# Attention's q·kv as three float32r products with a block-diagonal kv, partial sums kept in PSUM, and the maximum of k as a tree: one change to a Trainium2 kernel

## The chip, the cores and the metric

The kernel runs on one core of one Trainium2 chip. The metric is the device time of one execution in microseconds; shown are the median, the lowest and the highest of three runs. Engines are named as the profile names them: PE (matrix products), PEld (its weight loads), DVE (vector), ACT (scalar), POOL (GpSimd) and SP (which issues the DMAs).

## The reference

The kernel computes a linear attention whose softmax of q runs over the head dimension and whose softmax of k runs over the sequence, and then two feed-forward blocks. There are 8 batches of 8 heads, 576 positions and 64 head dimensions; 4608 tokens, a width of 512 and 2048 hidden units.

```
q_s = softmax(q, axis=-1); k_s = softmax(k, axis=2)
kv = np.einsum('bhsd,bhse->bhde', k_s, v)
attn = np.einsum('bhsd,bhde->bhse', q_s, kv)
x = attn.transpose(0, 2, 1, 3).reshape(B * S, H * D)
h = x @ w_in; x = (h * (1.0 / (1.0 + np.exp(-1.702 * h)))) @ w_out
h = x @ w_in2; out = np.maximum(0.01 * h, h) @ w_out2
```

## The kernel before

**Tiles and halves.** Tokens go in nine chunks of 512 (0 to 8). Matrix products of the two feed-forward blocks (`layer` 0 and 1) take float32r operands in two halves, a high and a low one: `split_hi` (L83) rounds on ACT, `split_lo` (L86) subtracts on DVE, and each product is a sum of three, high·high, low·high and high·low.

**Stages.** First, attention of chunk 0 in an order written out by hand (`FIRST`). Then a loop over the 16 tiles of hidden units (and five more turns) does the first matrix of layer 0 for chunks 0 and 1 (`g1`, L719), the second (`g2`, L789), and converts the weights, which come as 64-bit words (`c1` to `c4`). Attention of chunk 1 runs in its first turns, and chunks 2 and 3 in the turns after, one unit in two turns. Then come pairs of chunks (0,2), (0,4), (0,6), the single chunk (0,8), and layer 1 with the pairs (1,0), (1,2), (1,4), (1,6) and the single (1,8). A pair's first matrix is a product of 2 by 2 blocks with seven block products instead of eight (`quad_step`, and `quad_apart` from (1,2) on; L732): eight steps for a pair, 32 by `quad_step` and 24 by `quad_apart`. The second matrix is `g2`, or from (1,2) on seven rounds in `pair_apart` (L1056).

**A step of a pair.** It has three PSUM banks a, b and c (tag `h`, names `ha`, `hb`, `hc`). The products go, six matmuls each, in the order a = a11·w11; b = s2·t2; c = s1·t1; a += a12·w21; b += s3·t3; c += s4·w22; b += a22·t4. ACT copies a's first product to SBUF (`p1`), and DVE adds it to what later comes out of b and c, so a step has five DVE adds (L900 and its helper, L956 in `quad_apart`). Pieces of other work stand in ten gaps of a step.

**Attention in units.** A unit is a chunk and a pair of heads (c, j), four to a chunk; `Units.tick` puts its pieces into the gaps of three successive steps. `k1` takes k's maximum over rows with a reduction (L429), and with a further maximum for what is left over in chunk 0 (L431). `k6` multiplies k and v into the bank `kvp`, and `k7` divides by the sum on ACT into `kv` (L492), three buffers for each j. `q3` transposes the scaled q, `q4` copies it to `qT` (L540). `x_product` (L556) multiplies kv and qT: for each of the two heads a float32 matmul on a 64 by 64 quarter of the array, and since batches of 576 positions don't fall on chunks of 512, chunks 1 to 7 have two pieces each (64 and 448 columns in chunk 1, 128 and 384 in chunk 2, and so on). Chunks 0 and 8 have one piece of 512. From the pairs on, `kma`, `kmb`, `qtp`, `kvp` and `pxt` of the units share one PSUM bank (tag `att`).

**Order.** Each engine runs its queue in order. The order is set by a scheduler from the program's text; the gaps are where the text puts the pieces. The lines that call `x_product` stand in `tick`:

```
if c:
    at(0, x_product, *c)
    at(0, self.done, *c)
```

Of the kernel before, what the change touches and what calls it, by code (L numbers as in the profile page):

```python
# [26 lines left out]
def tile_softmax_linear_attention_two_mlps(  # L27
# [247 lines left out]
    def sums_hi(n):  # L275
        h = pool["wt"].tile([P, 4, 2 * P], F32R, tag="wt", name="wt", bufs=1)
        split_hi(sums[n][1], h)
        sums[n].append(h)

    def sums_lo(n):  # L280
        _, t, h = sums.pop(n)
        lo = t.bitcast(F32R)
        split_lo(t, h, lo)
        for i, half in enumerate((h, lo)):
            nc.sync.dma_start(out=wtd[:, :, n, i, :], in_=half.bitcast(F32))
# [111 lines left out]
    def load_first(p0):  # L397

        def slot(name):
            return p0.tile([P, 4 * T], F32, tag=name, name=name)  # L400
# [4 lines left out]
        va, vb = slot("va"), slot("vb")  # L405
# [20 lines left out]
    def k1(b, j):  # L426
        km, *rest = kin[b, j]
        mx = sb.tile([P, 2, D], F32, tag="kmx", name="kmx", bufs=2)
        nc.vector.tensor_reduce(out=mx, in_=km.rearrange("p h r d -> p h d r"), axis=AX.X, op=ALU.max)  # L429
        for kr in rest:  # L430
            nc.vector.tensor_tensor(out=mx, in0=mx, in1=kr, op=ALU.max)  # L431
        kst[b, j] = mx

# [52 lines left out]
    def k7(b, j):  # L486
# [29 lines left out]
    def q2(c, j):  # L516
        qt, sm = qin.pop((c, j)), qst[c, j]
        nc.vector.reciprocal(sm, sm)
        qs = sb.tile([P, R, 2, D], F32, tag="qs", name="qs", bufs=3)
# [17 lines left out]
    def q4(c, j):  # L537
        pt = qst.pop((c, j))
        t = sb.tile([P, T], F32, tag="qs", name="qT", bufs=3)
        nc.scalar.copy(t, pt)  # L540
        qT[c, j] = t
# [3 lines left out]
    def x_product(c, j):  # L545
        t = qT.pop((c, j)).rearrange("p (r c) -> p r c", r=R)
# [3 lines left out]
        while done < T:  # L550
# [3 lines left out]
            for h in range(2):  # L554
                o = slice(h * D, (h + 1) * D)
                nc.tensor.matmul(pv[o, :, a:e], kvb[b, j][o, :], t[o, :, a:e], start=True, stop=True)  # L556
# [284 lines left out]
    class Units:  # L841
# [8 lines left out]
        def tick(self):  # L850
# [8 lines left out]
            if c:  # L859
                at(0, x_product, *c)  # L860
                at(0, self.done, *c)
# [32 lines left out]
    def quad_step(layer, n, gaps, extra):  # L894
# [7 lines left out]
        a = ps.tile([P, T], F32, tag="h", name="ha", bufs=3)  # L902
# [608 lines left out]
```

## Time and profile before

| what | value |
|---|---|
| median of 3 runs | 1627.37 us (1627.02 to 1627.89) |
| profiled execution, its own time | 1628.65 us |
| its span, first to last instruction | 1626.9 us |
| PE busy | 1587.7 us, 98% of the span |
| DVE busy | 1053.7 us, 65% |
| ACT busy | 800.9 us, 49% |
| granted clock of PE, mean | 0.997 of full speed |

The profiled execution took 1.75 us more than its span, and 1.3 us more than the median. Busy time is the union of an engine's instructions. A matmul's end is modelled and overlaps the start of the next, so the durations of single matmuls are no price for one in a dense row: their distance from start to start is.

### The profile page before, as it was taken

What the parts mean: (1) busy time and instruction counts of PE and PEld (TensorE: products, weight loads), DVE (VectorE), ACT (ScalarE), POOL (GpSimd) and SP (SyncE); (2) the same over time, 40 slices, a digit from 0 to 9 for tenths busy, and PEclk for the clock granted to TensorE, in tenths of its full rate; (3) what the DMA queues carried; (4) which work ended last, traced back from release to release, by engine and by line L of the source; (5) the groups of instructions that cost most, each with busy time, mean ns of one, the idle gap of its engine ahead of it and who ended that gap; (6) DMA issues with size and microseconds to landing.
All of it is one profiled execution on the core that took longest, in us unless ns stands there. A gap on an engine that the chain in (4) does not pass through costs nothing.

```text
span 1626.9 us, 22121 instructions
## 1 busy us (share of the span) xinstructions
PE 1587.7 (98%) x7632; PEld 1268.3 (78%) x7632; DVE 1053.7 (65%) x1623; ACT 800.9 (49%) x1698; POOL 35.2 (2%) x162
## 2 busy tenths in 40 slices
PE   5999999999999999999999999999999999999998
PEld 3677778777877778778888888788888888888887
DVE  7899659786776757667544666644774487547411
ACT  7787656556545655445333545333453354334422
POOL 1000000000000002000000000000000000000000
PEclk9999999999999999999999999999999999999999
DMA  8788577778788887978896977996776777676763
GB/s 215 226 274 256 167 234 269 255 247 262 249 281 264 260 260 243 303 253 281 306 330 228 321 272 264 316 292 203 242 209 203 233 212 215 194 230 195 223 192 102
DMA packets 221775, 397.84 MB, mean 245 GB/s; under 512 B 57568, under 2 KB 138464, under 8 KB 221664
## 3 DMA queue, kind: packets, MB, share of 16 engines
q1 hardware_dynamic: 221664, 396.43, 76.1%
q8 instruction: 61, 1.00, 0.3%
q14 instruction: 50, 0.41, 0.1%
HBM read 306.18 MB, written 90.18 MB: 244 GB/s over the span
## 4 chain that ended last, share of the span: by engine, by line
PE 77%; DVE 7%; DMA 7%; issue 3%; ACT 1%; SPq 1%; ACTq 0%; DVEq 0%; POOL 0%; POOLq 0%
PE acc L789 23%; PE hb L732 13%; PE ha L732 9%; PE hc L732 8%; PE h L719 7%; PE ob L1056 6%; PE oa L1056 4%; PE oc L1056 4%; DMA o<-cv 2%; PE pxt L556 2%; DMA wo<-wp 1%; DMA w<-cv 1%; DVE cv L126 1%; DVE gl L86 1%; DMA raw<-in_moe_w_in_dram 1%
## 5 line engine op out<-in xcount | busy, mean ns | idle before, releaser
L789 PE MATMUL acc<-gh,wo 128*128 128x512 f32 x1152 | 362.8, 396 | 2.6 <-ACT wo L83 1.8
L789 PEld LDWEIGHTS acc<-gh,wo 128*128 128x128 f32 x1152 | 211.5, 188 | 48.9 <-ACT wo L83 2.2
L789 PE MATMUL acc<-gl,wo 128*128 128x512 f32 x576 | 225.6, 392 | 0.0
L719 PE MATMUL h<-x,wi 128*128 128x512 f32 x768 | 191.3, 399 | 2.8 <-ACT wi L83 2.8
L719 PEld LDWEIGHTS h<-x,wi 128*128 128x128 f32 x768 | 144.2, 191 | 37.2 <-ACT wi L83 4.4
L732 PE MATMUL ha<-x,wa 128*128 128x512 f32 x624 | 161.8, 393 | 2.8 <-ACT p L905 2.8
L732 PEld LDWEIGHTS ha<-x,wa 128*128 128x128 f32 x624 | 115.6, 188 | 33.0 <-issue 5.7
L83 ACT CAST sh<-a 128x1024 fp32r<-128x1024 f32 x84 | 88.2, 1050 | 94.4 <-PE oc L1056 35.1
L86 DVE TENSOR_TENSOR sl<-a,sh 128x1024 fp32r<-128x1024 f32 x84 | 102.7, 1222 | 49.4 <-ACT sh L83 49.0
L789 PEld LDWEIGHTS acc<-gl,wo 128*128 128x128 f32 x576 | 108.3, 188 | 23.8 <-issue 0.8
L956 DVE TENSOR_TENSOR a<-hb,a 128x512 f32<-128x512 f32 x72 | 49.7, 690 | 91.3 <-PE hb L732 91.3
L732 PE MATMUL hb<-x,wc 128*128 128x512 f32 x384 | 97.4, 389 | 0.0
L508 ACT ACTIVATE qt<-qt,qmx 128x64 f32<-128x64 f32 x256 | 86.0, 338 | 13.0 <-DVE qmx L498 12.2
L1056 PE MATMUL ob<-sh,wo 128*128 128x512 f32 x288 | 91.7, 394 | 0.0
L732 PE MATMUL hb<-xb,wb 128*128 128x512 f32 x336 | 86.1, 390 | 0.0
L83 ACT CAST gh<-gb 128x512 fp32r<-128x512 f32 x80 | 49.3, 617 | 71.8 <-PE acc L789 69.6
L732 PEld LDWEIGHTS hb<-x,wc 128*128 128x128 f32 x384 | 72.1, 188 | 14.9
L789 PE MATMUL acc<-wo,gh 128*128 128x512 f32 x256 | 79.2, 390 | 1.3 <-DMA wo<-wp 1.3
L83 ACT CAST gh<-gf 128x512 fp32r<-128x512 f32 x96 | 59.1, 616 | 42.5 <-DVE gf L757 33.6
L86 DVE TENSOR_TENSOR gl<-gb,gh 128x512 fp32r<-128x512 f32 x80 | 54.7, 687 | 35.5 <-ACT gh L83 34.2
L86 DVE TENSOR_TENSOR gl<-gf,gh 128x512 fp32r<-128x512 f32 x96 | 65.9, 687 | 18.0 <-ACT gh L83 17.1
L753 ACT ACTIVATE a<-a 128x512 f32<-128x512 f32 x72 | 45.5, 632 | 64.2 <-DVE a L956 64.2
(182 smaller groups left out, 2842.2 us busy)
## 6 DMA issues: line engine op xcount, KB each, us to landing
wo<-wo SPq DMA_DIRECT2D x144, 512.0 KB, 4.6
wo<-wp SPq DMA_DIRECT2D x68, 512.0 KB, 3.6
wo<-wt SPq DMA_DIRECT2D x48, 512.0 KB, 3.6
wa<-wq SPq DMA_DIRECT2D x40, 512.0 KB, 4.0
wb<-wq SPq DMA_DIRECT2D x40, 512.0 KB, 4.2
wc<-wq SPq DMA_DIRECT2D x40, 512.0 KB, 4.7
raw<-in_moe_w_in_dram SPq DMA_DIRECT2D x32, 512.0 KB, 4.9
raw<-in_moe_w_out_dram SPq DMA_DIRECT2D x32, 512.0 KB, 4.9
```

The lines of the kernel that those rows point to most:

```text
L83: nc.scalar.copy(hi, src)
L86: nc.vector.tensor_tensor(out=lo, in0=src, in1=hi.bitcast(F32), op=ALU.subtract)
L126: nc.vector.scalar_tensor_tensor(out=w[:, o], in0=hw, scalar=0xC0000000, in1=w[:, o], op0=ALU.bitwise_and, op1=ALU.bitwise_or)
L508: nc.scalar.activation(t[:, h, r, :], t[:, h, r, :], AF.Exp, bias=mx[:, h, r : r + 1], accum_out=sm[:, h, r : r + 1],)
L556: nc.tensor.matmul(pv[o, :, a:e], kvb[b, j][o, :], t[o, :, a:e], start=True, stop=True)
L719: nc.tensor.matmul(h, WI[f][:, b, wh, o * P : (o + 1) * P], xs[f"a{side}{b + 1}"][xh][:, o, :], start=(i == 0), stop=(i == n - 1),)
L732: nc.tensor.matmul(h, w[:, wh, o * P : (o + 1) * P], xo[xh][:, o, :], start=(start and i == 0), stop=(i == 5), skip_group_check=not start,)
L753: nc.scalar.activation(t, h, AF.Prelu, alpha=0.01)
L789: nc.tensor.matmul(acc[d], lhsT, rhs, start=(f == 0 and i == 0), stop=(f == NF - 1 and i == 2))
L956: add = lambda out, h, t: nc.vector.tensor_tensor(out=out, in0=h, in1=t, op=ALU.add)
L1056: nc.tensor.matmul(banks[name][d], w[:, l, wh, sl], x[:, l, :], start=first_one, stop=(m == NQ // 2 - 1 and l == 1 and i == 2), skip_group ...
```

## The change

Three things are changed.

**q·kv.** For chunk 0 all stays. For chunks 1 to 8, `k7` writes kv of two heads as the two diagonal blocks of a 128 by 128 tile, in a high half (two ACT instructions of 64 by 64) and a low half (two DVE instructions); eight such tiles (`kvt`, two batches by four j) are set to zero once by POOL. kv of batch 0, which chunk 1 needs too, is split by `k8` after `FIRST` (eight ACT and eight DVE instructions of 64 by 64). `q4` writes qT as a high half (ACT) and a low half (DVE). `x_product` is then three float32r matmuls over the whole array for each piece: high·high, low·high, high·low. In `tick` it moves from gap 0 to gap 1.

**Sums in PSUM.** In a step, ACT copies a's first product into bank b, in PSUM; the order of the next two is exchanged (c = s1·t1, then b += s2·t2), and b adds onto the copy. ACT then copies c and b to SBUF (`v5`, `u2`). Of the five DVE adds two remain; ACT has three copies instead of one. The seven rounds of `pair_apart` change in the same way. Three matmuls are added ahead of the first pair, one into each bank `h`.

**Maximum of k.** One reduction is replaced by a maximum of 256 elements, one of 128, and one of 128 for the rest.

Buffers are moved for room: the converted weights have three shared buffers (`cv`) instead of two and two; `qs` has two instead of three; the pool `wt` is gone, and `sums_hi` and `sums_lo` use the room of the new halves of qT, so the first does two ACT casts instead of one and the second three DMAs instead of two.

```diff
     def c1(i, f):
-        t = pool["cv"].tile([P, 2, T], U32, tag=f"cv{i}", name="cv", bufs=2)
+        t = pool["cv"].tile([P, 2, T], U32, tag="cv", name="cv", bufs=3)
...
     def k1(b, j):
         km, *rest = kin[b, j]
+        kr = rest[0] if rest else km[:, :, R, :]
         mx = sb.tile([P, 2, D], F32, tag="kmx", name="kmx", bufs=2)
-        nc.vector.tensor_reduce(out=mx, in_=km.rearrange("p h r d -> p h d r"), axis=AX.X, op=ALU.max)
-        for kr in rest:
-            nc.vector.tensor_tensor(out=mx, in0=mx, in1=kr, op=ALU.max)
+        two = sb.tile([P, 2, R // 2, D], F32, tag="km2", name="km2", bufs=1)
+        nc.vector.tensor_tensor(out=two, in0=km[:, :, 0 : R // 2, :], in1=km[:, :, R // 2 : R, :], op=ALU.max)
+        nc.vector.tensor_tensor(out=mx, in0=two[:, :, 0, :], in1=two[:, :, 1, :], op=ALU.max)
+        nc.vector.tensor_tensor(out=mx, in0=mx, in1=kr, op=ALU.max)
...
-        kv = sb.tile([P, D], F32, tag=f"kv{j}", name=f"kv{j}", bufs=3)
-        nc.scalar.activation(kv, pk[:, 0:D], AF.Copy, scale=rs)
-        kvb[b, j] = kv
...
+        hi, lo = kv_halves(b, j)
+        for h in range(2):
+            o, e = slice(h * D, (h + 1) * D), slice(h * D, (h + 1) * D)
+            nc.scalar.activation(hi[o, e], pk[o, 0:D], AF.Copy, scale=rs[o, :])
+            nc.vector.scalar_tensor_tensor(
+                out=lo[o, e], in0=pk[o, 0:D], scalar=rs[o, :], in1=hi.bitcast(F32)[o, e],
+                op0=ALU.mult, op1=ALU.subtract,
+            )
...
+    def k8(j):
+        hi, lo = kv_halves(0, j)
+        for h in range(2):
+            o, e = slice(h * D, (h + 1) * D), slice(h * D, (h + 1) * D)
+            split_hi(kvb[0, j][o, :], hi[o, e])
+            split_lo(kvb[0, j][o, :], hi[o, e], lo[o, e])
...
+        hi, lo = (sb.tile([P, T], F32R, tag=f"qT{i}", name=f"qT{i}", bufs=1) for i in "hl")
+        split_hi(pt, hi)
+        split_lo(pt, hi, lo)
+        qT[c, j] = hi, lo
...
+                hi, lo = kv_halves(b, j)
+                for i, (w, m) in enumerate(((hi, qh), (lo, qh), (hi, ql))):
+                    nc.tensor.matmul(pv[:, :, a:e], w, m[:, :, a:e], start=(i == 0), stop=(i == 2))
...
-                at(0, x_product, *c)
-                at(0, self.done, *c)
+                at(1, x_product, *c)
+                at(1, self.done, *c)
...
         product(a, "a11", W["w11"], True)
-        p1 = pool["cv"].tile([P, T], F32, tag="p1", name="p1", bufs=2)
-        nc.scalar.copy(p1, a)
+        nc.scalar.copy(b, a)
         run(gaps[1])
-        b = ps.tile([P, T], F32, tag="h", name="hb", bufs=3)
-        product(b, "s2", W["t2"], True)
-        u2 = pool["cv"].tile([P, T], F32, tag="u2", name="u2", bufs=2)
-        add(u2, b, p1)
-        run(gaps[2])
-        c = ps.tile([P, T], F32, tag="h", name="hc", bufs=3)
         product(c, "s1", W["t1"], True)
         v5 = pool["cv"].tile([P, T], F32, tag="v5", name="v5", bufs=2)
-        add(v5, c, p1)
+        nc.scalar.copy(v5, c)
+        run(gaps[2])
+        product(b, "s2", W["t2"], False)
+        u2 = pool["cv"].tile([P, T], F32, tag="u2", name="u2", bufs=2)
+        nc.scalar.copy(u2, b)
         run(gaps[3])
...
         product(b, "a22", W["t4"], False)
-        add(p1, b, p1)
         t21 = new_g(2, f0)
-        act1(layer, p1, t21)
+        act1(layer, b, t21)
...
+    hi = XO["a11"][0]
+    for i in range(3):
+        h = ps.tile([P, T], F32, tag="h", name="hp", bufs=3)
+        nc.tensor.matmul(h, hi[:, 0, 0:P], hi[:, 0, :], start=True, stop=True)
```

PE's queue in a step of the pair (0,2), where chunk 4's first unit reaches `x_product` (`ha`, `hb`, `hc` are the banks a, b, c; `pxt` is the product's bank; `kma` and `kmb` are transposes of the next unit's maximum). Before:

```order
L556 MATMUL pxt<-qT,kv_2313 64x4x64 x2
L556 MATMUL pxt<-qT,kv_3314 64x4x64 x2
L732 MATMUL ha<-x,wa 128x512 x6
L732 MATMUL hb<-xb,wb 128x512 x6
L446 MATMUL kma<-ident,kmx 128x128
L732 MATMUL hc<-x,wb 128x512 x6
L732 MATMUL ha<-x,wa 128x512 x6
```

And now, where `qTh` and `qTl` are the halves of qT, and `kvt_146` and `kvt_142` hold both halves of kv of two batches:

```order
L778 MATMUL ha<-x,wa 128x512 x6
L602 MATMUL pxt<-qTh,kvt_146 128x4x64 x2
L602 MATMUL pxt<-qTl,kvt_146 128x4x64
L602 MATMUL pxt<-qTh,kvt_142 128x4x64 x2
L602 MATMUL pxt<-qTl,kvt_142 128x4x64
L778 MATMUL hc<-x,wb 128x512 x6
L456 MATMUL kma<-ident,kmx 128x128
L778 MATMUL hb<-xb,wb 128x512 x6
L778 MATMUL ha<-x,wa 128x512 x6
```

The unit's product has moved behind a's first product, only c's product stands between a's first and b's first, and one product instead of two stands between `pxt` and `kma`.

ACT's queue at the second step of the pair (0,4) (`cv` is a tile of converted weights, `gb` and `gf` are activated hidden units). Before:

```order
L109 ACTIVATE cv_4790<-raw_4755 128x512
L112 ACTIVATE cv_4790<-raw_4755 128x512
L751 ACTIVATE gb<-p_4766 128x512
L905 COPY p_4911<-ha 128x512
L751 ACTIVATE gf<-ha 128x512
```

And now:

```order
L109 ACTIVATE cv_4999<-raw_4965 128x512
L112 ACTIVATE cv_4999<-raw_4965 128x512
L797 ACTIVATE gb<-hb 128x512
L950 COPY hb<-ha 128x512
L954 COPY v_5138<-hc 128x512
L958 COPY u_5152<-hb 128x512
L797 ACTIVATE gf<-ha 128x512
```

The copy of a stays behind the same conversion; two more copies have come between it and the activation of a.

## Rows read from the trace of the kernel before

**Rows 1.** The chain of work that ended last: page's shares, then a piece (start, us)
```profile
PE 77%; DVE 7%; DMA 7%; issue 3%; ACT 1%; SPq 1%; ACTq 0%; DVEq 0%; POOL 0%; POOLq 0%
...
818.54 2.72 PE h L719 x12
```

**Rows 2.** Windows: length, busy us of PE, PEld, DVE, ACT, POOL; clock, DMA
```profile
60.00:90.00 30.00, 27.58 (x155) 18.93 (x154) 28.77 (x57) 24.57 (x72) 1.52 (x10) 0.94 0.78 235
90.00:160.00 70.00, 67.06 (x335) 52.08 (x335) 67.26 (x133) 53.33 (x121) 2.40 (x11) 1.00 0.84 268
160.00:250.00 90.00, 89.51 (x521) 68.06 (x519) 58.27 (x102) 56.98 (x180) 4.84 (x31) 1.00 0.68 210
250.00:440.00 190.00, 190.00 (x1008) 149.83 (x1007) 150.08 (x251) 112.90 (x296) 6.40 (x41) 1.00 0.79 256
```

**Rows 3.** Tile pxt: its readers on ACT from chunk 2 on, ns min/median/max, first and last start
```profile
L587 ACT COPY xr<-pxt x28: 564/587/589, 130.0 to 717.9; 128x512 f32<-128x512 f32 x28
```

**Rows 4.** PE's timeline round a unit of chunk 4: start us, us, what, how many
```profile
303.39 0.39 PE L789 MATMUL acc<-gl,wo 128*128 128x512 f32 x1
303.71 1.08 PE L556 MATMUL pxt<-qT,kv 64*64 64x256 f32 x8
304.72 1.65 PE L732 MATMUL ha<-x,wa 128*128 128x512 f32 x6
306.21 1.52 PE L732 MATMUL hb<-xb,wb 128*128 128x512 f32 x6
```

**Rows 5.** Four transposes of 128 columns: PE's timeline; their group (busy, mean ns)
```profile
1211.26 0.60 PE L1004 MATMUL otp<-ident,u 128*128 128x128 f32 x4
...
L1004 PE MATMUL otp<-ident,u 128*128 128x128 f32 x24 | 3.8, 280 | 0.0
```

**Rows 6.** PE's waits for kv: the sum (us, times, longest), then three in the timeline
```profile
PE pxt L556 <- ACT kv L492: 5.5, 7, 1.4
...
495.19 1.08 PE L556 MATMUL pxt<-qT,kv 64*64 64x384 f32 x8 [1.12 <-ACT kv L492]
...
513.70 1.08 PE L556 MATMUL pxt<-qT,kv 64*64 64x384 f32 x8 [0.54 <-ACT kv L492]
...
550.75 1.08 PE L556 MATMUL pxt<-qT,kv 64*64 64x448 f32 x8 [1.19 <-ACT kv L492]
```

**Rows 7.** A quiet step: PE's second product, and ACT's copy of the first
```profile
324.11 1.52 PE L732 MATMUL hb<-xb,wb 128*128 128x512 f32 x6
...
324.36 0.59 ACT L905 COPY p<-ha 128x512 f32<-128x512 f32 x1 [1.04 <-PE ha L732]
```

**Rows 8.** A late copy: PE's wait for it, and what ACT waited for
```profile
462.54 1.66 PE L732 MATMUL ha<-x,wa 128*128 128x512 f32 x6 [2.42 <-ACT p L905]
...
460.29 0.66 ACT L109 ACTIVATE cv<-raw 128x512 uint32<-128x512 uint32 x1 [5.26 <-DMA w<-cv]
```

**Rows 9.** DVE groups by form: count, busy us, mean ns, idle before
```profile
L429 DVE TENSOR_REDUCE kmx<-kt 128x128 f32<-128x640 f32 x28 | 36.3, 1296 | 15.2 <-DMA kt<-in_k_dram 15.0
L431 DVE TENSOR_TENSOR kmx<-kmx,va 128x128 f32<-128x128 f32 x4 | 1.1, 286 | 0.0
L602 DVE TENSOR_TENSOR t<-w,t 128x256 f32<-128x256 f32 x16 | 6.7, 420 | 0.2
L86 DVE TENSOR_TENSOR x<-pxt,x 128x512 fp32r<-128x512 f32 x8 | 5.5, 685 | 0.2 <-ACT x L83 0.2
L489 DVE TENSOR_SCALAR krs<-kvp 128x1 f32<-128x1 f32 x32 | 4.8, 150 | 3.0 <-PE kvp L477 2.9
```

**Rows 10.** ACT groups by form: count, busy us, mean ns, idle before
```profile
L905 ACT COPY p<-ha 128x512 f32<-128x512 f32 x32 | 18.6, 581 | 12.3 <-PE ha L732 12.1
L492 ACT ACTIVATE kv<-kvp,krs 128x64 f32<-128x64 f32 x32 | 9.5, 304 | 9.1 <-DVE krs L490 9.1
L83 ACT CAST sh<-a 128x1024 fp32r<-128x1024 f32 x84 | 88.2, 1050 | 94.4 <-PE oc L1056 35.1 <-PE ob L1056 30.4 <-PE oa L1056 28.8
```

**Rows 11.** POOL's groups by form: the nearest memset
```profile
L348 POOL MEMSET va<- 64x256 f32 x2 | 0.6, 306 | 0.1
```

More of the change, by code (lines that the diff above doesn't have):

```diff
@@ L553, in x_product @@
             a, e = done // R, (done + n) // R
-            for h in range(2):
-                o = slice(h * D, (h + 1) * D)
-                nc.tensor.matmul(pv[o, :, a:e], kvb[b, j][o, :], t[o, :, a:e], start=True, stop=True)
+            if c == 0:
+                for h in range(2):
+                    o = slice(h * D, (h + 1) * D)
+                    nc.tensor.matmul(pv[o, :, a:e], kvb[b, j][o, :], t[o, :, a:e], start=True, stop=True)
+            else:
+                hi, lo = kv_halves(b, j)
+                for i, (w, m) in enumerate(((hi, qh), (lo, qh), (hi, ql))):
+                    nc.tensor.matmul(pv[:, :, a:e], w, m[:, :, a:e], start=(i == 0), stop=(i == 2))
             done += n
@@ L962, in quad_apart @@
         run(gaps[0])
-        a = ps.tile([P, T], F32, tag="h", name="ha", bufs=3)
+        a, b, c = (ps.tile([P, T], F32, tag="h", name=f"h{x}", bufs=3) for x in "abc")
         product(a, "a11", W["w11"], True)
-        nc.scalar.copy(t21, a)
+        nc.scalar.copy(b, a)
         run(gaps[1])
-        b = ps.tile([P, T], F32, tag="h", name="hb", bufs=3)
-        product(b, "s2", W["t2"], True)
-        add(t12, b, t21)
+        product(c, "s1", W["t1"], True)
+        nc.scalar.copy(t22, c)
         run(gaps[2])
-        c = ps.tile([P, T], F32, tag="h", name="hc", bufs=3)
-        product(c, "s1", W["t1"], True)
-        add(t22, c, t21)
+        product(b, "s2", W["t2"], False)
+        nc.scalar.copy(t12, b)
         run(gaps[3])
@@ L987, in quad_apart @@
         product(b, "a22", W["t4"], False)
-        add(t21, b, t21)
-        act1(layer, t21, t21)
+        act1(layer, b, t21)
         run(gaps[8])
@@ L1047, in pair_apart @@
             name = "acabbcb"[r]
-            if m == 0 and r in (0, 1, 3):
+            if m == 0 and r < 2:
                 banks[name] = acc2(name)
@@ L1087, in pair_apart @@
                 else:
-                    add(p1[d], h[d], p1[d])
-                    out_part(c + 1, d, p1[d])
+                    t = pool["cv"].tile([P, T], F32, tag="ev", name="ev", bufs=4)
+                    nc.scalar.copy(t, h[d])
+                    out_part(c if r == 2 else c + 1, d, t)
     def pair_first(layer, c, units, held, work):
@@ L1177, in tile_softmax_linear_attention_two_mlps @@
         named[word[:2]](int(word[2:]))
+    for t in kvt.values():
+        nc.gpsimd.memset(t.bitcast(F32), 0.0)
+    for j in range(NP):
+        k8(j)
     p0.release()
@@ L1430, in tile_softmax_linear_attention_two_mlps @@
             held = pair_second(layer, c + 1, steps)
-            if nxt == (0, LAST):
-                take("left", "wt")
             if layer == 1:
@@ L1437, in tile_softmax_linear_attention_two_mlps @@
                 sb.release()
-                give("wt", "cv", "lo")
+                give("cv", "lo")
                 take("left", "lo", "cv")
```

81 lines of the change are left out of this document (49 added, 32 removed).

## The prediction

> **What bounds the kernel now.** I read the chain of waits first: PE holds 77% of it, and the rest is spread over DVE, DMA and small shares [rows 1]. Shares are means over stages, so the windows come next. From 160 us on PE is full: 89.51 of 90 us, then 190.00 of 190 us, while DVE has 150.08 and ACT 112.90 of those 190 [rows 2]. There only three things move the end: the length of PE's own row, PE's waits, and work that stands alone at the ends. From 60 to 160 us PE and DVE are equally full: 27.58 and 28.77 of 30 us, then 67.06 and 67.26 of 70 us [rows 2]. There a shorter row of PE buys little and a longer row of DVE may cost. The granted clock is 1.00 in these windows, 0.94 from 60 to 90 us; I forecast no change in it. A dense row of 128 by 512 float32r matmuls has its price in the chain: 2.72 us for twelve, 0.2267 us each [rows 1], so a product of six is 1.36 us.
>
> The sum is made against the profiled execution, 1628.65 us, which is 1.3 us above the median, 1627.37 us; the difference that it gives is then taken from the median.
>
> **The change part by part.**
>
> *1. q·kv on PE.* Before, chunk 4's unit stands between two rows of products: from the last `acc` product (303.39) over `pxt` (303.71) and the next row's start (304.72) to the row after (306.21) are 2.82 us, of which seven are dense products, 7 × 0.2267 = 1.59 [rows 4]. The unit costs 1.23 us; by columns alone a unit of any chunk has 512 of them, and I take 1.23 for all. Now it is three float32r products over each piece. A column of a dense product costs 0.2267/512 us. For short pieces the nearest row is four transposes of 128 columns: the first is 280 ns and all four are 0.60, so 0.32 for three, a floor of 0.11 us each [rows 5]. The price of a product is the larger of the two. A unit of chunks 1 and 7 (64 and 448 columns) is 3 × (0.11 + 0.198) = 0.92 us; of 2 and 6 (128 and 384) 0.84; of 3 and 5 (192 and 320) 0.76; of 4 and 8 0.68. The savings are 0.31, 0.39, 0.47 and 0.55 us. Only those where PE is the bound count. The first reader of `pxt` from chunk 2 on starts at 130.0 us [rows 3], and chunks 2 and 3 have a unit in two turns, so I count the last two units of chunk 2 and all of chunks 3 to 8: 2 × 0.39 + 4 × (0.47 + 0.55 + 0.47 + 0.39 + 0.31 + 0.55) = **−11.7 us**. The six units before would save 2.0 us more, which I leave out.
>
> The packed form of before costs 1.23 us for 512 columns, and three dense products over the whole array 0.68, so the row speaks for the block-diagonal form. The Trainium skill, "TensorEngine Tiling (Array Packing)", "When to Use Tiling", speaks against it: a contraction of 64 is what packing is for, and here half of the array is filled with zeros. By that rule alone the float32r products would be better packed too; no row shows such a form, and its gain would not be this change's.
>
> *2. PE's waits for kv.* PE waits 5.5 us in seven places for kv, and in the full stretch 1.12, 0.54 and 1.19 us, together 2.85 [rows 6]. `x_product` now stands one product (1.36 us) later. The chain to it grows: kv was one ACT instruction of 0.304 us [rows 10], and is now two, then two on DVE, each no less than DVE's smallest here, 0.150 us [rows 9]; some 0.6 us more. The move gains 0.76 us net: min(1.12, 0.76) + 0.54 + 0.76 = **−2.05 us**, between 0 and −2.85.
>
> *3. a's copy into PSUM.* In a quiet step ACT's copy starts at 324.36 and takes 0.59 us, so it ends at 324.95; PE's second product starts at 324.11, and that product is now c's, so b's would start at 325.47 [rows 7]. 0.5 us of cover in each of the 56 steps: **0**. Behind b's wait on PE all the rest of the step is queued, and DVE and ACT behind that. Not all steps are quiet. In the pair (0,4) ACT stands 5.26 us before a conversion (L109) that waits for a DMA, with the copy behind it, and PE waits 2.42 us [rows 8]. PE wanted the copy only before its fourth row; now before the third, one product earlier. Two such steps and half of one where the wait is new would be 2.5 × 1.36 = 3.4; DVE's add, which used to follow, no longer stands in between, so I take **+2.5 us**, between 0 and 5.
>
> The two further copies of a step (0.58 us each, [rows 10]) stand ahead of ACT's next activations, and on the shared bank only one product is left between `pxt` and the next unit's `kma`; ACT must read `pxt` in it, 0.587 us [rows 3], perhaps behind a copy of 0.581: 1.17 of 1.36 us. Mostly covered; **+1.5 us**, between 0 and 4. The three DVE adds that go, and the second DVE instruction of qT, whose wait on ACT's half holds up DVE's adds behind it, meet a DVE with 40 us of 190 idle [rows 2]: 0. The three added matmuls are 3 × 0.2267 = **+0.7 us**.
>
> *4. DVE before 160 us.* A unit gets the low half of qT, 0.685 us by the row of that shape, and two small instructions, between 0.150 and 0.286 each, say 0.4 in all; the maximum of k was 1.296 us and becomes 0.42 + 2 × 0.286 = 0.99 [rows 9]. Net +0.77 us, in six units +4.7. `k8` adds eight small instructions, 1.6; chunk 0's four maxima give back 4 × 0.31. Together 5.0 us, if DVE is the bound throughout. It has 1.2 and 2.7 us idle in the two windows, and PE 2.4 and 2.9 [rows 2]; I take **+3 us**, between 0 and 5. The shared buffers of the weights (three for four) lie within that.
>
> *5. The start.* `k8` puts eight ACT casts, at most 0.304 us each [rows 10], ahead of chunk 1, and POOL gets eight memsets, near 0.306 us each [rows 11], in a time when POOL is idle. The tree shortens the first maximum: **+0.75 us**, between −1 and 2.5.
>
> *6. Layer 1 and the rest.* `sums_hi`, `sums_lo`, the further DMA on SP's queue and the copies of `pair_apart` stand beside a full PE: ACT's casts of 128 by 1024 (1.05 us, [rows 10]) have 94 us of idle time ahead of them, which ended with a bank coming from PE: 0.
>
> Sum: −11.7 − 2.05 + 2.5 + 1.5 + 0.7 + 3 + 0.75 = **−5.3 us**, from 1627.4 to **1622 us**.
>
> **The rivals.**
>
> *Short float32r products are dear.* No row has a float32r product of fewer than 512 columns. If those under 256 columns cost per column what float32 did in `pxt`, 1.01 us for 512 (303.71 to 304.72, [rows 4]), the three products of a short piece cost 0.38, 0.76 and 1.14 us at 64, 128 and 192 columns. The savings become 0.26 for chunks 1 and 7, −0.04 for 2 and 6, −0.33 for 3 and 5, and stay 0.55 for 4 and 8; the first term is then 4 × 0.66 − 0.08 = 2.6 us instead of 11.7, and the time 1631. For it: float32 is slow here by the column. Against it: the transposes, at 0.11 us, are float32 and short.
>
> The Trainium skill, "TensorE: Matmul & The Clock Gate", "Back-to-back issue gap", gives about 81 ns for a product of 128 columns with its weight load. Put in place of 0.11 us for the 72 short products, it would give some 2 us more gain by estimate; the transposes' 0.11 us is the trace's, and no run here yet shows another.
>
> *ACT's write into PSUM is slow.* No row has ACT writing PSUM. The copy to SBUF takes 0.581 us, and twice the elements 1.050 [rows 10]; I take 0.58, since the reading side is the same. The cover of a step ends when it takes more than 1.1 us (324.36 to 325.47, [rows 7]); from there every 0.1 us costs 56 × 0.1 = 5.6 us. At 1.3 us it is +11, 1633, at 1.4 us 1639: slower than before. Against it: twice the elements to SBUF stay below 1.1 us, so a write to PSUM would have to cost as much as a copy of twice its size.
>
> The Trainium skill, "ScalarE: Activation LUTs", "Step-by-step: what each stage is for", holds ScalarE's writes to PSUM for faster than those to SBUF; by it this rival falls. No run here shows it yet.
>
> *Everything hidden but PE's row.* If DVE in the first stage only follows PE, the copies are covered, and ACT's late copies are met by DVE's relief, then the six early units save too and all three waits for kv go: −11.7 − 2.0 − 2.85 + 0.7 = −15.9, **1611.5**. For it: PE is the engine named most in the chain [rows 1]; against it, DVE's 67.26 of 70 us [rows 2].
>
> That the change does not do what it says is not likely: the number of dense products is the same in both programs, and q·kv's new form is plain in PE's queue.
>
> **How the numbers follow.** Forecast 0.50, its own range 1616 to 1628 by the bounds of the terms; short products dear 0.20; slow write 0.15; all hidden 0.15. The range 1612 to 1633 leaves out half of the last two and the top of the second. About 0.2%, 3.25 us, is what a measurement of this kernel can tell from no change: faster is below 1624.1, slower above 1630.6. The forecast gives 0.35 to faster, 0.13 to no change and 0.02 to slower; dear short products 0.10 and 0.10; the slow write 0.01 and 0.14; all hidden 0.15 to faster. So 0.50, 0.24 and 0.26.
>
> **What the profile after would show.** Term 1: PE's row without `pxt` is 0.7 to 0.9 us shorter than with it; over 1.2 for chunks 2, 3, 5 and 6 is the first rival. Term 2: no wait of `pxt` for kv after 160 us. Term 3: ACT's copy into `hb` near 0.58 us, and PE's waits for it only near 460 and 650 us; a wait in every step is the second rival. Term 4: from 60 to 160 us DVE fuller and the first pair later by 2 to 5 us; if it starts no later, the third. I am wrong altogether if the clock falls below 1.00 after 160 us, or if layer 1, which I hold at zero, gets shorter or longer by more than 2 us.

## The result: slower by 0.6%, and where the time went

| | before | after |
|---|---|---|
| median of 14 runs, us | 1627.36 | 1636.08 |
| lowest to highest | 1624.93 to 1628.99 | 1630.12 to 1645.18 |
| profiled execution / its span | 1628.65 / 1626.9 | 1640.06 / 1638.3 |

The ratio is 1.006 [1.0044, 1.0076]: 8.7 us slower, where I had forecast 5.3 us faster. Executions of the changed kernel lie further apart than those of before, and the profiled one is 4 us above its median (that of before 1.3 above), so some 2.7 of the 11.4 us between the two traces are the execution's and not the kernel's. How far a single stretch can move between executions stands in step 4.

The totals of the page after (busy time, share of the span, instructions) tell nothing of the loss:

```profile
PE 1588.1 (97%) x7575; PEld 1286.8 (79%) x7575; DVE 961.5 (59%) x1601; ACT 880.2 (54%) x1872; POOL 34.5 (2%) x170
```

PE is busy as long as before (1587.7 us), DVE 92 us less and ACT 79 us more. So PE has 11 us more of waiting, and the question is where. I took the start of the n-th of the 6432 dense products (the 512-column matmuls of the feed-forward blocks) in both traces; the growth of the difference is what each stretch lost or gained. A seam is the place where one pair of chunks gives way to the next pair or single chunk:

| stretch, by the clock of before | difference at its end, us | lost (+) or gained (−) | my sum had |
|---|---|---|---|
| start, to the first product at 30.3 us | +5.25 | +5.25 | +0.75 |
| product 801, at 266.8 | +10.71 | +5.5 | +1.0 |
| product 2701, at 760.1: the pairs of layer 0 | +3.75 | −7.0 | −7.1 |
| product 2901, at 806.6: the seam at (0,8) | +7.82 | +4.1 | 0 |
| product 3901, at 1033.3 | +7.84 | 0.0 | 0 |
| product 4101, at 1080.7: the seam at (1,2) | +10.49 | +2.65 | 0 |
| product 6401, at 1615.3 | +11.38 | +0.9 | 0 |

"My sum had" sorts the prediction's terms into these stretches: +1.0 is DVE's +3 and the three added matmuls' 0.7 (they run ahead of the 801st product), less 2.66 for the units of chunks 2 and 3; −7.1 is 9.1 for the units of chunks 4 to 8 and 2.05 for kv, against 2.5 + 1.5. The steady stage came out as summed, but not term by term. By the costs of a unit below, q·kv alone saves 8.4 us there; PE's waits for kv fell only from 2.9 to 2.7 us, and by the rest of the −7.0 the copies cost some 1.6 us instead of 4.0. Two errors of 2 us offset each other, which is luck. In this execution all of the loss is outside that stage, where I had put little or nothing.

**The unit of chunk 4**, PE's timeline of after, which answers to [rows 4] (start, time, engine, line, operation, tiles, shapes, count):

```profile
313.91 1.53 PE L778 MATMUL ha<-x,wa 128*128 128x512 f32 x6
315.28 0.40 PE L602 MATMUL pxt<-qTh,kvt 128*128 128x256 f32 x2
315.51 0.28 PE L602 MATMUL pxt<-qTl,kvt 128*128 128x256 f32 x1
315.63 0.39 PE L602 MATMUL pxt<-qTh,kvt 128*128 128x256 f32 x2
315.86 0.28 PE L602 MATMUL pxt<-qTl,kvt 128*128 128x256 f32 x1
315.98 1.54 PE L778 MATMUL hc<-x,wb 128*128 128x512 f32 x6
```

From 315.28 to 315.98 are 0.70 us for six short products. Against rows of dense products without them, a unit for which PE doesn't wait costs 0.72 us in chunk 4, 0.79, 0.88 and 0.95 in 5, 6 and 7, and 0.71 in 8 (mine: 0.68, 0.76, 0.84, 0.92, 0.68).

**The copies**, groups of after (busy time and mean ns, then idle time ahead and what ended it), for [rows 9, 10]:

```profile
L950 ACT COPY hb<-ha 128x512 f32<-128x512 f32 x32 | 18.3, 572 | 19.7 <-PE ha L778 19.3
L954 ACT COPY v<-hc 128x512 f32<-128x512 f32 x32 | 18.6, 582 | 19.9 <-PE hc L778 19.9
L509 ACT ACTIVATE kvt<-kvp,krs 64x64 fp32r<-64x64 f32 x56 | 17.3, 308 | 31.9 <-DVE krs L500 23.6 <-DVE kvt L510 7.8
L510 DVE SCALAR_TENSOR_TENSOR kvt<-kvp,krs,kvt 64x64 fp32r<-64x64 f32 x56 | 15.7, 281 | 9.3 <-ACT kvt L509 8.6
```

ACT's write into PSUM takes 572 ns, its write of a tile of the same shape to SBUF 582 ns.

**PE's waits** of after (total, times, longest), for [rows 6, 8]:

```profile
PE kma L456 <- DVE kmx L436: 9.6, 3, 8.9
PE pxt L602 <- DVE kvt L510: 2.8, 5, 0.9
PE ha L778 <- DMA wa<-wq: 2.7, 1, 2.7
PE pxt L602 <- ACT kvt L509: 2.5, 3, 1.5
PE acc L835 <- ACT gh L83: 2.0, 1, 2.0
PE hb L778 <- ACT hb L950: 1.4, 3, 0.9
```

The waits for the halves of kv are as long in sum (5.3 us) as those for kv were before (5.5). The waits for `wa` by DMA and for `gh` are new.

**The start.** In `q3`, chunk 0's qT was always taken from the buffers of `qs`, of which the change leaves two instead of three. Now `qs` of a further j waits until a unit's product has read qT. DVE, then ACT, of after:

```profile
22.22 0.69 DVE L551 TENSOR_TENSOR qs<-q,qsm 128x512 f32<-128x512 f32 x1 [1.72 <-PE pxt L598]
...
26.90 0.59 ACT L572 COPY qT<-qtp 128x512 f32<-128x512 f32 x1 [3.57 <-PE pxt L598]
```

And PE behind them:

```profile
31.90 3.68 PE L598 MATMUL pxt<-qT,kv 64*64 64x512 f32 x8 [1.53 <-ACT kv L503]
35.51 0.72 PE L765 MATMUL h<-x,wi 128*128 128x512 f32 x2
```

Dense products begin at 35.5 us instead of 30.3. The last eight short products of chunk 0 also take 3.68 us; before, they took 1.94, and 1.7 of the 5.25 us are that (see the last section).

**The seam at (0,8).** A pair of layer 0 also converts weights: pieces of `conv_step` stand in gaps 3, 6 and 8, a load by DMA, ACT's L109 and L112, and DMAs on. ACT in that pair of after:

```profile
753.68 0.58 ACT L950 COPY hb<-ha 128x512 f32<-128x512 f32 x1
754.19 1.04 ACT L83 CAST x<-xr 128x1024 fp32r<-128x1024 f32 x1
755.22 0.59 ACT L954 COPY v<-hc 128x512 f32<-128x512 f32 x1
756.58 0.59 ACT L958 COPY u<-hb 128x512 f32<-128x512 f32 x1 [0.77 <-PE hb L778]
757.06 0.67 ACT L109 ACTIVATE cv<-raw 128x512 uint32<-128x512 uint32 x1
```

The conversion of gap 3 now stands behind three copies that wait for PE. What hangs on it (a DMA, the next conversion, the weights' load) can come later by that; the trace was not followed link by link, and e7 below moves this piece. 47 us on, ACT stands still before a conversion that waits for a DMA, with the cast for `acc` queued behind it, and then PE waits:

```profile
804.12 0.66 ACT L109 ACTIVATE cv<-raw 128x512 uint32<-128x512 uint32 x1 [5.28 <-DMA o<-cv]
804.68 0.65 ACT L112 ACTIVATE cv<-raw 128x512 f32<-128x512 f32 x1
805.23 1.13 ACT L83 CAST gh<-gb 128x512 fp32r<-128x512 f32 x2
...
805.88 0.70 PE L835 MATMUL acc<-gh,wo 128*128 128x512 f32 x2 [2.04 <-ACT gh L83]
```

The wait is half of the +4.1 us. Behind it the granted clock is 0.50, the lower of its two levels (1.2 of 2.4 GHz); columns as in [rows 2]:

```profile
806.95:810.36 3.41, 3.41 (x10) 2.67 (x9) 1.80 (x3) 0.31 (x1) 0.00 (x0) 0.50 0.75 251
```

Dense products follow each other at 0.43 us there instead of 0.2267, which costs some 1.6 us by estimate. The trace of before has no such fall after 160 us. The prediction named a clock below 1.00 after 160 us as a sign of being wrong altogether; it came, behind a wait at a seam.

**The seam at (1,2).** SP's queue, which issues the DMAs in order, after:

```profile
1074.74 3.60 SPq L858 DMA_DIRECT2D out_dram<-ev  x4
1078.43 0.38 SPq L297 DMA_DIRECT2D wa<-wq  x1
```

and before:

```profile
1063.51 0.32 SPq L294 DMA_DIRECT2D wa<-wq  x1
...
1067.48 3.60 SPq L812 DMA_DIRECT2D out_dram<-ev  x4
```

This load takes a buffer that is free when the step's third product has run: at 1063.3 us before, at 1071.4 in after. Before, it stood ahead of the four output DMAs (0.9 us each) and was issued at once; now it stands behind them, 7 us after its buffer came free. No line of the diff moves it. The scheduler sets the queue's order, and with the new step it came out another way; why, the runs don't show. PE pays:

```profile
1085.21 1.62 PE L778 MATMUL ha<-x,wa 128*128 128x512 f32 x6 [2.74 <-DMA wa<-wq]
```

### The profile page after: what moved, and what is told of

Same layout as the page of the kernel before. It is cut to its first block, busy times and chain, and to the rows that moved or that the text cites. A ratio compares the mean times of both kernels' runs of the same rounds, so it can differ in the third digit from the quotient of the medians.

```text
span 1638.3 us, 22211 instructions
## 1 busy us (share of the span) xinstructions
PE 1588.1 (97%) x7575; PEld 1286.8 (79%) x7575; DVE 961.5 (59%) x1601; ACT 880.2 (54%) x1872; POOL 34.5 (2%) x170
## 5 line engine op out<-in xcount | busy, mean ns | idle before, releaser
L998 DVE TENSOR_TENSOR a<-hb,a 128x512 f32<-128x512 f32 x24 | 16.6, 692 | 156.6 <-PE hb L778 156.6
L778 PE MATMUL hb<-xb,wc 128*128 128x512 f32 x288 | 74.7, 395 | 0.3 <-ACT u L958 0.3
L778 PEld LDWEIGHTS hb<-xb,wb 128*128 128x128 f32 x336 | 62.1, 188 | 16.3 <-ACT hb L950 3.1
```

Source lines behind the costliest of these rows:

```text
L778: nc.tensor.matmul(h, w[:, wh, o * P : (o + 1) * P], xo[xh][:, o, :], start=(start and i == 0), stop=(i == 5), skip_group_check=not start,)
L998: add = lambda out, h, t: nc.vector.tensor_tensor(out=out, in0=h, in1=t, op=ALU.add)
```

## The experiments

Ratios are against runs of the kernel before on the same chip (medians 1627.0 to 1628.4). "After" is 1636.08. Differences between two experiments are of medians, in part from different chips; where they are under some 3 us the spread of executions covers them, and PE's waits in the traces carry the reading. A trace is of one execution.

**e1: chunk 0's qT in a buffer of its own.** Everything else as after.

```diff
-            t = sb.tile([P, T], F32, tag="qs", name="qT", bufs=2)
+            t = sb.tile([P, T], F32, tag="qT" + "hl"[j % 2], name="qT", bufs=1)
```

> The changed kernel, but in chunk 0 qT stands in the rooms of the two halves of qT, which chunk 0 does not use, and no longer shares the two buffers of qs. Theory 1 (the buffer taken from qs holds up chunk 0): the first dense product starts at about 30.3 us as before instead of 35.6, PE's second unit no longer waits behind its own bank, and the time falls by about 5 us to 1631. Rival (the start is late because of the added splits k8 and their place on ACT): the first dense product still starts after 34 us and the time stays near 1636.

1630.26 us, ratio 1.0015 [1.0001, 1.0029]: 5.8 us less than after. PE's timeline of e1 has the dense products back at 30.2 us, and the eight short products at 1.93:

```profile
28.37 1.93 PE L598 MATMUL pxt<-qT,kv 64*64 64x512 f32 x8 [0.96 <-ACT qT L572]
30.23 0.73 PE L765 MATMUL h<-x,wi 128*128 128x512 f32 x2
```

The taken buffer is the whole loss of the start and, by the medians, two thirds of the loss of the kernel. The place is steady across the traces: e3 and e4, which keep the shared buffer, begin 4.3 and 4.9 us late, e1 and all other runs at most 0.9.

**e2: the sums in PSUM alone**, on the kernel before: the steps, the rounds and the three added matmuls; q·kv, gaps and the maximum as before.

```diff
-        nc.scalar.copy(p1, a)
+        nc.scalar.copy(b, a)
...
-        add(u2, b, p1)
-        add(v5, c, p1)
+        nc.scalar.copy(v5, c)
+        nc.scalar.copy(u2, b)
```

> The kernel before with the sums in PSUM alone (steps, rounds and the three added matmuls); q.kv and the maximum of k as before. Theory 1 (the price lies in q.kv's buffers and in the first 260 us): 1625 to 1630, as before. Rival (the copies of a step and their queue on ACT are the price): 1633 or more, with PE waiting for the copy into bank b in many steps.

1641.69 us, 1.0079 [1.006, 1.0098]: 14 us slower, though its copy takes 573 ns and the dense rows are unchanged. PE's waits of e2:

```profile
PE pxt L556 <- ACT kv L492: 6.6, 6, 1.5
PE acc L789 <- DMA wo<-wo: 5.0, 2, 2.5
PE ha L732 <- DMA wa<-wq: 3.8, 1, 3.8
PE acc L789 <- DMA wo<-wp: 2.7, 2, 1.6
```

By the n-th product it loses 6.0 us from 760 to 807 us and 7.8 from 1033 to 1081, the two seams; the profiled execution is the slowest of six, 4 us above the median. The wait for `wa` is only half of the 7.8. In its last 1.5 us the granted clock falls to the lower level and stays there for 6.8 us, with products 0.43 us apart, some 3 us more by estimate:

```profile
1086.85:1093.67 6.82, 5.33 (x13) 4.20 (x14) 0.00 (x0) 0.57 (x1) 0.00 (x0) 0.50 0.83 305
```

The sums bring the seams' losses with them.

**e3: the maximum of k as one reduction again**, in after.

```diff
-        nc.vector.tensor_tensor(out=two, in0=km[:, :, 0 : R // 2, :], in1=km[:, :, R // 2 : R, :], op=ALU.max)
-        nc.vector.tensor_tensor(out=mx, in0=two[:, :, 0, :], in1=two[:, :, 1, :], op=ALU.max)
+        nc.vector.tensor_reduce(out=mx, in_=km.rearrange("p h r d -> p h d r"), axis=AX.X, op=ALU.max)
```

> The changed kernel with the maximum of k as a reduction again. Theory 1: the tree is worth little, 0 to 3 us on a DVE that is full before 160 us, so 1636 to 1639. Rival (the tree's three instructions, with the buffer that they share, hold up the next unit): 1633 or less.

1640.26 us, 1.0073 [1.0057, 1.0088]: 4 us above after, whose interval, [1.0044, 1.0076], overlaps. No harm of the tree shows, so the rival falls; that it is worth 4 us isn't shown.

**e4: `x_product` back in gap 0**, in after.

```diff
-                at(1, x_product, *c)
-                at(1, self.done, *c)
+                at(0, x_product, *c)
+                at(0, self.done, *c)
```

> The changed kernel with q.kv's product at gap 0 again, ahead of a's first product. Theory 1 (kv's halves end last there): PE waits for kv's halves 1.4 us longer in the three steps of the pairs where it waits now and in others, together 4 us or more, so 1640. Rival (the move costs more by the bank that it shares with the next unit than it saves): 1634 or less.

1650.29 us, 1.0128 [1.0111, 1.0145]: 14 us slower than after, where I had put 2 us on the move. The wait for the low half, e4:

```profile
PE pxt L602 <- DVE kvt L510: 9.5, 8, 2.6
```

against 2.8 us in after. So the chain to the halves is far longer than the 0.9 us at which I had priced it; and the 6.7 us more of this wait are only half of the 14. Longer waits for `wo`, `wa` and `hb` are a part of the rest; the profiled execution is the slowest of five, 6 us above the median.

**e5: the sums in layer 1 alone** (the rounds and the steps without `x_product`), on the kernel before.

> The kernel before with the sums in PSUM in layer 1 alone (the apart steps, the rounds, the three added matmuls). The run with the sums alone lost about 14 us, 2 x 0.8 of them at the starts of the pairs (1,4) and (1,6), where a transpose waits for ACT's copy, and none within the dense rows of layer 1. Theory 2 (the price is made by the steps of layer 0 and (1,0), which move the order of the queues, and is paid at the seams): 1628 to 1630, and the first steps of (1,2) wait for no weights. Rival (the copies into PSUM are dear in every step): 24 steps of the apart form cost 4 us or more, 1632 or more.

1630.58 us, 1.0022 [1.0007, 1.0037]. No wait for `wa`; PE waits twice for 0.7 us at the starts of pairs, for ACT's copy of an output part that now stands behind another copy. One of the two, e5:

```profile
1226.13 0.66 PE L1001 MATMUL otp<-ident,ev 128*128 128x128 f32 x4 [0.70 <-ACT ev L1082]
```

Layer 1's part is small but not nought.

**e6: output parts of chunk 1 on POOL's queue**, e1 otherwise.

```diff
-        nc.sync.dma_start(out=dst, in_=t)
+        (nc.gpsimd if layer and c == 1 else nc.sync).dma_start(out=dst, in_=t)
```

> The run with chunk 0's qT in its own room, and the four DMAs that store chunk 1's output go out of POOL's queue instead of SP's; nothing else moves. There the load of wa for the second step of (1,2) stands behind these four on SP, which wait for the last sums, and PE waits 2.1 to 4.2 us for wa in all runs with the sums. Theory 2 (SP's order): wa is issued some 6 us earlier, the wait goes, 2 us or more off the 1630.3 us. Rival (the load is late because its slot is late): wa is issued at the same distance to PE's third product, and the wait stays.

1627.98 us, 1.0001 [0.9989, 1.0013]: 2.3 us less than e1; the intervals overlap, and the wait decides. By the n-th product the seam at (1,2) lost 2.4 us in e1 and gains 1.4 here. PE's wait for `wa`, e1 and then e6:

```profile
1079.29 1.62 PE L778 MATMUL ha<-x,wa 128*128 128x512 f32 x6 [1.73 <-DMA wa<-wq]
```

```profile
1082.69 1.62 PE L778 MATMUL ha<-x,wa 128*128 128x512 f32 x6 [0.18 <-DMA wa<-wq]
```

**e7: the first piece of a conversion in gap 1**, ahead of the copies of c and b; e1 otherwise.

```diff
-                for i, piece in zip((3, 6, 8), conv_step()):
+                for i, piece in zip((1, 6, 8), conv_step()):
```

> The run with chunk 0's qT in its own room, and in the steps of the pairs of layer 0 the first piece of a conversion stands in gap 1 instead of gap 3, ahead of the copies of c and b on ACT. Theory 2 (the added copies hold up the conversions behind them, and with them a chain of DMAs that ends in PE's waits near 772 and 799 us, 3 to 6 us together): these waits fall below 2 us together, and the time by 2 us or more to 1628. Rival (the conversion now waits for its DMA ahead of the copies, and PE behind them): waits for the copy into bank b of over 1 us in several steps, 1633 or more.

1628.41 us, 1.0005 [0.9991, 1.0018]: 1.9 us less than e1. In e1 PE waited 2.2 and 1.9 us for `wo` at the seam (0,8), here 0.3 and 1.3. The time by itself isn't clear of the spread, but by the n-th product the seam's loss falls from 3.5 us in e1 to 1.1. That queue was a cause of it.

**e8: kv's halves in two tiles, both ACT instructions ahead of both of DVE**; e1 otherwise.

> The run with chunk 0's qT in its own room, and kv's two halves in two tiles, ACT's two instructions first and then DVE's two. In the changed kernel ACT's second waits 0.34 us for DVE's first, a chain of 1.4 us to PE instead of the 0.9 that I had put. Theory (that chain ends last where PE waits for kv): PE's waits for kv's halves after 160 us fall by 0.3 to 0.5 us each, some 2 us in all, 1628. Rival (what ends last there is the wait for the sum of k, the same in both): less than 1 us, 1630.

1631.13 us, 1.002 [1.0004, 1.0035], no better than e1. The longest wait for a low half falls from 2.3 to 0.8 us, the sum from 4.9 to 3.1, and the time doesn't follow. A gain of some 2 us could hide in the spread; none shows.

**e9: e1 without the sums** (the steps and rounds of before; for room `u2` and `v5` have one buffer each).

> The run with chunk 0's qT in its own room, with the sums of before (five adds on DVE, one copy on ACT in a step); q.kv in halves and the tree stay. For room, the temporaries u2 and v5 of a step have one buffer each, and the stores of layer 0 share all four temporaries. Theory 2 (q.kv saves what the working says, and the sums take it away at the seams): near 1618, between 1614 and 1622; no wait for a copy into a bank, no wait for wa at (1,2). Rival (the two parts are not additive: q.kv's units themselves move the seams): 1626 or more.

1627.25 us, 1.0002 [0.9993, 1.0012]: outside the range of the theory and in that of the rival. But the rival's reason isn't what the trace shows: it loses nothing at the seams (+0.2 us at (0,8), −1.8 at (1,2)). That execution, 1622.8 us, is the fastest of twelve. The waits for the low half remain (3.3 us in four places), and 3.4 us come back before `ha`, which waits for ACT's copy as in [rows 8]. The single buffers are a handicap of this kernel, and how much of it is theirs I can't say.

**e10: the queues mended together**: e1, e6, e7, and of the two copies of round 6, for which pair starts wait (e5), one on DVE.

```diff
-                    nc.scalar.copy(t, h[d])
+                    (nc.vector.tensor_copy if r == 6 and d else nc.scalar.copy)(t, h[d])
```

> All edits to the queues together, with the sums in PSUM: chunk 0's qT in its own room, chunk 1's output stored from POOL's queue, the conversions' first piece in gap 1, and at the end of a pair's rounds the second copy on DVE instead of ACT. Theory 2 (each removes a wait of its own): 1630.3 less 2.3, 1.9 and 1.2 gives 1625, between 1623 and 1627. Rival (they remove the same wait, or the next wait takes its place): 1628 or more.

**1623.35 us, 0.9966 [0.9953, 0.9978]: faster than both kernels.** It is 6.9 us below e1. e6 and e7 give 4.2 of them by themselves; the other 2.7 are the DVE copy's, come of the three together or lie in the spread, which wasn't told apart. The kept trace is of its slowest execution, 1630.65 us, so no place in it is read here.

**e11 and e12: `x_product` later still**, in gap 3 or gap 2 of a pair, with `k2` and `k3` of the next unit behind it; e10 otherwise. Of e11:

```diff
-                at(1, x_product, *c)
+                at(3 if late_pools else 1, x_product, *c)
-                    at(2, k2, *b)
-                    at(2, k3, *b)
+                    at(4 if late_pools else 2, k2, *b)
+                    at(4 if late_pools else 2, k3, *b)
```

> The run with all edits to the queues, and in the pairs q.kv's product in gap 3 instead of 1 (behind c's and b's products), the next unit's transposes of the maximum in gap 4. Theory 3 (the chain to kv's halves, which stands on DVE behind a conversion that waits for ACT, ends 1 to 3 us after the product is due): PE's waits for the halves between 440 and 660 us, 5 us together, go, and the time falls by 2 to 5 us to between 1618 and 1621. Rival (the next unit's chain, which now starts later, waits at its own places instead): no gain, 1623 or more.

> As the run with gap 3, but with the product in gap 2 and the transposes in gap 3; the queue then has the product where it was or one product later, and only the transposes are one product later. Theory 3: the waits for kv's halves stay, the waits of the transposes for the shared bank (some 1 us) go, 1622 to 1624. Rival: as with gap 3, 1620 or less.

1628.59 us, 0.9999 [0.9986, 1.0013], and 1626.67 us, 0.9982 [0.9968, 0.9996]: neither is faster than e10, e11 is slower, and e12's interval overlaps with e10's, [0.9953, 0.9978]. e11 still waits for the low half:

```profile
PE pxt L602 <- DVE kvt L510: 4.8, 6, 1.7
```

The theory that a later product would be free of the waits fell. That the next unit's chain starts later by what its predecessor's product was moved, and so passes the waits on, follows from the program's order and wasn't shown.

**e13: e2 with `x_product` in gap 1.**

> The run with the sums alone, with the float32 q.kv product in gap 1 instead of 0. Theory 2 (the sums are paid at the seams, near 776, 805 and 1084 us, 10 us together): 1638 or more, as the run with the sums alone. Rival (they are paid where PE waits for kv, since ACT's copies stand ahead of it, as the changed kernel with gap 0 lets expect): 1633 or less.

1636.41 us, 1.0064 [1.0051, 1.0078]: 5.3 us less than e2, between what the theory and the rival asked for. By the medians some 5 of the 14 us of the sums alone lie in the place of q·kv's product, and 9 are left; the two intervals overlap. The seams' waits are among them, here at (1,2):

```profile
PE ha L732 <- DMA wa<-wq: 3.6, 1, 3.6
```

**e14: e10 with q·kv as it was before** (packed float32, kv whole).

> The run with all edits to the queues, without q.kv's new form: float32 product of two quarters in gap 1, kv and qT in one part, the buffers of before. The sums and the tree stay. Theory 1 (term 1 of the working is real: 11 us on PE's row, 4 to 6 of them lost again in waits for kv's halves): 1628 to 1631, 5 to 7 us above the 1623.35 us with q.kv's halves. Rival (the waits take the whole gain): 1624 or less.

1631.37 us, 1.0024 [1.0012, 1.0037]: 8.0 us above e10, clear of the spread. That is what q·kv's new form, with the buffers that were moved for it, is worth where the queues are mended.

**e15: e9 with the mends of e6 and e7.**

> The run without the sums (q.kv's halves, the tree, chunk 0's qT in its own room, the sums of before, one buffer each for u2 and v5), with the two edits to the queues that also concern it: chunk 1's output stored from POOL's queue, the conversions' first piece in gap 1. Theory (the sums buy nothing on a full PE, and what is left of their cost beside the repairs is some 4 us): 1620 to 1624. Rival (the adds that the sums take from DVE shorten the chain to kv's halves, so they are worth more than they cost beside q.kv's new form): 1626 or more, above the 1623.35 us of all edits together.

1625.91 us, 0.999 [0.9975, 1.0004], 2.6 us above e10, which has the sums. With the single buffers of e15, no DVE copy in it and intervals that touch, that shows the sums to be neither a gain nor a loss. Against e9 it is 1.3 us less, within the spread: with the sums of before, the mends of e6 and e7 have no clear effect.

## Why the prediction was wrong, point by point

**What bounds the kernel** was right: PE's row and PE's waits moved the end, and behind some waits PE's clock. Three things failed: the start had no term for the buffer taken from `qs` (step 5); the chain to kv's halves was priced by durations, 0.9 us where 5.2 pass (step 2); and the terms for the copies and for layer 1 (steps 3 and 6) looked at durations under a full PE and not at the order of the queues, so that the seams at (0,8) and (1,2) stood at nothing.

**Step 1, q·kv: right in size.** 0.71 to 0.95 us a unit against my 0.68 to 0.92. The units of chunks 5 and 6 for which PE doesn't wait stay under 0.9 us, where the rival of dear short products needed more than 1.2, so it fell. The Trainium skill's 81 ns for a product of 128 columns ("TensorE: Matmul & The Clock Gate", "Back-to-back issue gap") isn't what the trace shows: a piece of three products of 128 columns holds up the dense row behind it by 0.34 us, 0.11 each, the floor taken from the transposes [rows 5]. (My 2 us for that figure counted 72 short products; 18 of them are in the six early units that the term leaves out.) e14 against e10 is 8.0 us for the block-diagonal form, where the rule of the Trainium skill, "TensorEngine Tiling (Array Packing)", "When to Use Tiling", would pack a contraction of 64. But the two forms differ in number type too, float32 against float32r, so no run here tests that rule by itself. The 8.0 are fewer than the 11.7 of the term; that the longer chain and DVE's work (steps 2 and 4) take the difference was not measured apart.

**Step 2, the waits for kv: wrong, twice.** I priced the chain by the durations of its instructions, 0.9 us. In the pair around 520 us, timelines of PE, DVE, ACT and PE again, it is this:

```profile
517.38 0.80 PE L487 MATMUL kvp<-vt,kt 128*64 128x65 f32 x20
...
519.41 0.43 DVE L116 TENSOR_SCALAR cv<-cv 128x512 f32<-128x512 f32 x1 [1.15 <-ACT cv L112]
519.75 0.15 DVE L499 TENSOR_SCALAR krs<-kvp 128x1 f32<-128x1 f32 x1
520.50 0.15 DVE L500 RECIPROCAL krs<-krs 128x1 f32<-128x1 f32 x1
...
521.08 0.30 ACT L509 ACTIVATE kvt<-kvp,krs 64x64 fp32r<-64x64 f32 x1
...
522.96 0.29 DVE L510 SCALAR_TENSOR_TENSOR kvt<-kvp,krs,kvt 64x64 fp32r<-64x64 f32 x1
...
523.39 0.59 PE L602 MATMUL pxt<-qTh,kvt 128*128 128x384 f32 x2 [0.89 <-DVE kvt L510]
```

5.2 us from the end of `kvp` to the product, of which the instructions shown are 1.3. The rest is queueing: DVE stands 1.15 us before a conversion's add, and on ACT four exponentials stand ahead of the first half (521.08) and three more ahead of the second (522.39). So waits remained after 160 us, against what I had said the profile would show. And the move to gap 1, which I had at 0.76 us net, is worth 14 (e4): at gap 0 PE stops for the low half in seven units between 267 and 760 us, six of them among the eight of chunks 6 and 7.

**Step 3, a's copy into PSUM: the place I looked at was right, the cost lay elsewhere.** The copy takes 572 ns, so the rival of a slow write fell; here the trace agrees with the Trainium skill ("ScalarE: Activation LUTs", "Step-by-step: what each stage is for"), which holds PSUM for the faster side: 572 against 582 ns. PE's waits for `hb` are 1.4 us in three places, where I took 2.5 for late copies. But I asked only what stands behind PE's wait, and not what stands behind the copies on ACT: a conversion, a DMA, and the weights of the seam 47 us later. The seam at (0,8) lost 4.1 us: waits of 2.7 us, where before had 0.7, and the stretch at the lower clock. By the medians e7 takes 1.9 away.

**Step 4, DVE before 160 us: the sign that I gave didn't show, and the size stays open.** The stretch from 30 to 267 us lost 5.5 us, and I had 1.0. DVE isn't fuller: 27.26 of 30 and 65.74 of 70 us against [rows 2], and PE has 22.83 of 30 at a granted clock of 0.89. Windows of after, columns as in [rows 2]:

```profile
60.00:90.00 30.00, 22.83 (x140) 17.34 (x140) 27.26 (x65) 20.84 (x63) 2.39 (x14) 0.89 0.72 219
90.00:160.00 70.00, 67.53 (x335) 54.00 (x334) 65.74 (x136) 53.84 (x133) 2.23 (x11) 1.00 0.79 250
160.00:250.00 90.00, 86.44 (x500) 68.51 (x499) 65.00 (x145) 60.09 (x190) 5.51 (x31) 1.00 0.68 216
```

From 160 to 250 us PE has 86.44 of 90 us, where it was full before. But 5.5 us is one execution's figure. In e1, e6, e7 and e10 every engine has the same instructions in the same order up to 267 us, and their traces lose 4.3, 0.4, 1.3 and 2.4 us in this stretch. In e1 one wait of 2.34 us for a low half, up to 241.8 us, and a fall of the clock make most of the difference; e6 has neither. The window of e1:

```profile
241.40:244.80 3.40, 3.00 (x10) 2.74 (x11) 2.58 (x6) 3.38 (x15) 0.00 (x0) 0.50 0.88 283
```

So a term of +3 can be neither confirmed nor refuted by one trace. e3, with the longer reduction on DVE, loses 5.5 us here as after does, so its trace doesn't show DVE's path to count either. What lengthened this stretch in after stays open.

**Step 5, the start: the largest miss that a run settles.** I had a term for instructions, +0.75 us, and none for the buffer. That `qs` has two instead of three stood among the changes; I never followed who else draws on that tag: +5.25 us in the trace, 5.8 by e1.

**Step 6, layer 1 at nought: wrong by 3.5 us.** A full PE and idle ACT cover durations, but not an order. With the new step the load of `wa` came to stand behind four DMAs on SP's queue (e6: 2.3 us), and pair starts got two waits of 0.7 us (e5).

**The rivals.** None of the three happened. The case that did, in which queues and a taken buffer cost more than q·kv gains, was not among them. With the edges mended (e10) the kernel is 4.2 us faster than before, near the 5.3 of the sum. That is no proof of the sum: the mends of e6 and e7 were not tried on the kernel before. In e15 against e9, which have its steps and rounds, they gave 1.3 us, within the spread.

## What to carry to other kernels

Where an engine is full, price an edit's duration from the steady stage, but look for its loss at the seams: follow, for each instruction that moves, what stands behind it on every queue (the DMA-issuing ones too) up to the next stage's first load. A buffer taken from a shared tag is a term of its own, with all users of that tag listed. And the length of a chain is read from its end-to-end time in the trace of a nearby chain, with the queues that it crosses, not from its instructions' durations.

## What the runs showed of the hardware

Three things I had not expected.

Eight short float32 products ran in 3.68 us in after and in 1.93 in e1, the ratio of the two levels of the clock (1.2 and 2.4 GHz), while the granted clock reads 1.00 for both in the window from 20 to 36 us. That 1.00 is no reading: the trace's records of the clock begin with its rise, at 35.5 us in after, at 19.5 in e1 and at 20.4 in before, and a window ahead of the first record counts as full. Ahead of the rise after's short products and transposes take twice as long (four transposes 1.12 us against 0.63). So the late start of the dense products goes with a late rise of the clock; why it rose later wasn't tried. Later it falls again at three of PE's long waits: the one that ends at 805.88 us in after (2.04 us), at 241.80 in e1 (2.34) and at 1088.34 in e2 (3.84). There a wait costs more than its own length.

Float32r products of 64, 128 and 192 columns cost about 0.11 us each, as float32 transposes of 128 do, once the dense row behind them is counted up to its steady spacing; single starts lie 0.03 to 0.11 us apart. Those of 256 columns follow each other at 0.117.

Executions of one program lie apart by very different amounts: 15 us for after, 4 us for before in the same comparison, 11 us for before in e15's. A part of that arises in the first 267 us, where traces with the same order of instructions differ by 4 us (step 4); where the rest arises wasn't found.
